# Agent attention with two expert layers: w_in decoded in M's place, decoding begun earlier, keys loaded first, the last block in halves

## The chip, the cores and the metric

The kernel runs on one core of one Trainium2 chip. The metric is the device time of one execution in microseconds (us), as a median of runs. The core has TensorE (matrix products), VectorE (DVE in the rows), ScalarE (ACT), GpSimd (POOL) and SyncE (SP). TensorE writes to PSUM only; 16 DMA engines bring data from the chip's memory, and loads are issued here by SP, by ScalarE or by GpSimd. The clock granted to TensorE has two levels, 1.2 and 2.4 GHz; the profile gives it as a share of the upper one.

## What is computed

The inputs are fp32, but the weights of the expert layers are 64-bit numbers, which the kernel turns into pairs of fp32r numbers (high and low) on the chip. N is 12480 tokens, C is 128 channels, there are 49 agents, and the layers are 2048 wide.

```
a2k = softmax(agents @ k.T / sqrt(128))        # 49 x 12480
agent_v = a2k @ v                              # 49 x 128
x = softmax(q @ agents.T / sqrt(128)) @ agent_v
h = maximum(x @ w_in, 0);   x = (s * h * h + b) @ w_out
h = maximum(x @ w_in2, 0);  out = (h * h) @ w_out2
```

The kernel uses that `x @ w_in` is `softmax(q agents) @ (agent_v @ w_in)`. The 49-row product M = agent_v @ w_in is made once. The high and low parts of the softmax stand in 113 rows of one tile (49 rows, a gap up to row 64, 49 rows), and M stands twice in the same way, so that one product with 113 live rows does both parts.

## The kernel before

The program has a prologue and a main loop. All engines get their instructions in the order in which they are written, and each engine works through its own in that order.

*Loads at the start.* SP loads the agents; ScalarE issues two broadcasts of one number each to 128 partitions, s and b (lines 380 to 382). Then the string `FIRST` (line 24) gives the order of the first loads on SP: `k` is a piece of 1024 keys of 512 KB, `w` a raw block of a weight, also 512 KB, which goes to one of `RAW` = 4 buffers.

*Keys.* There are 13 pieces (the last of 192 keys). In step g of the loop, piece g is transposed on TensorE and copied by ScalarE (`k_transpose`), the load of a later piece is issued, the scores of piece g-1 are made on TensorE and copied by ScalarE (`k_scores`), and a running maximum is taken on VectorE (`k_max`). `KB` = 5 is the number of buffers for keys.

*Decoding.* Each of the four weights has four raw blocks of 512 columns, 16 in all. `w_decode` turns one into a high and a low fp32r tile: one activation on ScalarE reads the raw words, seven instructions follow on VectorE, and a late cast on ScalarE writes the high half. `fill(n)` issues n of these steps, taking two blocks in turn, and when a block is finished it issues the load of a next one on GpSimd's queue. `FILL_K`, `FILL_T`, `FILL_V`, `FM` and `FILL_L` say how many steps stand at which place: per key step, in the softmax's constants, per step of the attention sum, around M's first two pieces, and per step of the main loop. `finish(n)` issues what is missing until n blocks are left.

Here w_in is decoded into the tile of the fourth weight, w_out2 (`wi = wo2_f`). So a block of w_out2 may be decoded only when the piece of M that reads the same columns has been made (`made`).

*Attention sum and M.* 104 products over the key pieces give the sum over v (`ps_av`), while VectorE shifts and ScalarE exponentiates the scores. Then follow in a chain: the reciprocal of the softmax's sum, the scaled sum, its transposition, high and low copies of it (`av`), and M in four pieces of 512 columns (`m_piece`): three products on TensorE, a cast on ScalarE, a subtraction on VectorE. Two pieces stand ahead of the main loop, two in its steps 2 and 3.

*Main loop.* There are 28 blocks of 448 tokens (the last has 384) and eight steps for each block. A step has `up1` (four matmuls with M), `down` of the first layer two steps later, and, eleven steps later, `up2` and the second `down`, six matmuls each. After each `up`, `hidden` does ReLU and square on ScalarE, then the high copy and the low subtraction on VectorE (`split`). The first eleven steps have no second layer yet. At the end of a block, `y2_done` copies the result, `store` transposes it on TensorE, copies it on VectorE and issues the store on SP.

## Time and profile before

| | us |
|---|---|
| runs, three: median (lowest to highest) | 1141.26 (1140.69 to 1141.89) |
| profiled execution | 1140.76 |
| its span in the trace | 1138.8 |
| TensorE busy | 1119.6 |
| VectorE busy | 968.0 |
| ScalarE busy | 944.9 |

The span runs from the first to the last instruction of the trace; the profiled execution's own time is 1.96 us longer. A matmul's busy time includes what overlaps with the next one, so a busy TensorE is not one at its peak. Rows name an instruction by the line of the code, the tile that it writes and the tiles that it reads, and in square brackets the idle time of the engine before it with what ended it.

### The profile page before, as it was taken

How to read it: one execution, taken by the hardware profiler on the slowest of the kernel's cores; microseconds unless marked ns; L12 is line 12 of the kernel's file. 1: busy time of each engine (PE TensorE's matmuls, PEld its weight loads, DVE VectorE, ACT ScalarE, POOL GpSimd, SP SyncE). 2: the span in 40 equal slices, each digit the busy share in tenths (PEclk: the TensorE clock that was granted, in tenths of full speed). 3: DMA queues.
4: the chain of work that ended last, by engine and by line, in shares of the span. 5: the costliest groups of instructions: out<-in, count | busy, mean ns of one | idle time of the engine just before them, and what ended most of it. 6: DMA issues, size and time to landing. Idle time of an engine off the chain costs nothing.

```text
span 1138.8 us, 15466 instructions
## 1 busy us (share of the span) xinstructions
PE 1119.6 (98%) x5787; PEld 1022.8 (90%) x5787; DVE 968.0 (85%) x1426; ACT 944.9 (83%) x1186; POOL 12.7 (1%) x36
## 2 busy tenths in 40 slices
PE   8998999999999999999999999999999999999998
PEld 8886999999999999999999999999999999999997
DVE  4989888888888888888888888888888888888875
ACT  5657888888888888888888888888888888888875
POOL 2110000000000000000000000000000000000000
PEclk8899999999999999999999999999999999999999
DMA  8960019999999999999999999999999999700000
GB/s 318 287 182 1 1 17 8 15 15 15 7 15 15 15 8 15 15 15 10 12 15 15 15 8 15 15 15 8 15 15 15 8 15 15 11 1 9 9 10 15
DMA packets 1282658, 34.96 MB, mean 31 GB/s; under 512 B 1255239, under 2 KB 1277656, under 8 KB 1282584
## 3 DMA queue, kind: packets, MB, share of 16 engines
q1 hardware_dynamic: 1280568, 27.69, 114.4%
q0 software_dynamic: 1728, 6.29, 1.7%
q8 instruction: 45, 0.74, 0.4%
q14 instruction: 29, 0.24, 0.1%
q10 hardware_dynamic: 288, 0.00, 0.0%
HBM read 27.58 MB, written 6.39 MB: 30 GB/s over the span
## 4 chain that ended last, share of the span: by engine, by line
PE 94%; DVE 3%; DMA 1%; issue 1%; ACT 1%; SPq 0%; DVEq 0%; ACTq 0%
PE ps_y L579 47%; PE ps_h L568 24%; PE ps_h L558 15%; PE ps_av L508 2%; PE ps_o L606 1%; PE ps_sT L179 1%; PE ps_ks L426 1%; DMA raw<-in_moe_w_out_dram 1%; DMA kraw<-in_k_dram 1%; DVE gl L115 1%; PE ps_x L225 0%; PE ps_k L416 0%; DVE gh L114 0%; PE ps_b L194 0%; PE ps_s L169 0%
## 5 line engine op out<-in xcount | busy, mean ns | idle before, releaser
L115 DVE TENSOR_TENSOR gl<-r,gh 128x896 fp32r<-128x896 f32 (+1 forms) x448 | 487.4, 1088 | 15.4
L545 ACT ACTIVATE r<-ps_h 128x896 f32<-128x896 f32 (+1 forms) x448 | 408.0, 911 | 110.3 <-PE ps_h L558 90.4
L546 ACT ACTIVATE r<-r 128x896 f32<-128x896 f32 (+1 forms) x448 | 425.9, 951 | 14.2
L114 DVE CAST gh<-r 128x896 fp32r<-128x896 f32 (+1 forms) x448 | 279.2, 623 | 120.7 <-ACT r L546 115.7
L568 PE MATMUL ps_h<-yh,wi2l 128*128 128x448 f32 (+1 forms) x448 | 167.9, 375 | 1.8 <-ACT e L202 1.7
L558 PE MATMUL ps_h<-X,Ml 128*128 128x448 f32 (+1 forms) x448 | 166.1, 371 | 3.0 <-DVE X L236 2.2
L579 PE MATMUL ps_y<-gl,woh 128*128 128x448 f32 (+1 forms) x448 | 164.6, 368 | 0.7 <-DVE gl L115 0.7
L579 PE MATMUL ps_y<-gh,wol 128*128 128x448 f32 (+1 forms) x448 | 164.9, 368 | 0.0
L579 PE MATMUL ps_y<-gl,wo2h 128*128 128x448 f32 (+1 forms) x448 | 163.8, 366 | 0.6 <-DVE gl L115 0.6
L579 PE MATMUL ps_y<-gh,woh 128*128 128x448 f32 (+1 forms) x448 | 164.4, 367 | 0.0
L568 PE MATMUL ps_h<-yh,wi2h 128*128 128x448 f32 (+1 forms) x448 | 163.8, 366 | 0.0
L579 PE MATMUL ps_y<-gh,wo2l 128*128 128x448 f32 (+1 forms) x448 | 163.8, 366 | 0.0
L568 PE MATMUL ps_h<-yl,wi2h 128*128 128x448 f32 (+1 forms) x448 | 163.4, 365 | 0.1
L558 PE MATMUL ps_h<-X,Mh 128*128 128x448 f32 (+1 forms) x448 | 163.5, 365 | 0.0
L579 PE MATMUL ps_y<-gh,wo2h 128*128 128x448 f32 (+1 forms) x448 | 162.4, 362 | 0.0
L558 PEld LDWEIGHTS ps_h<-X,Ml 128*128 128x128 f32 x448 | 84.7, 189 | 11.1 <-issue 3.8
L579 PEld LDWEIGHTS ps_y<-gl,woh 128*128 128x128 f32 x448 | 84.4, 188 | 9.1 <-DVE gl L115 1.2
L579 PEld LDWEIGHTS ps_y<-gh,wol 128*128 128x128 f32 x448 | 84.4, 188 | 8.5 <-ACT y L587 0.4
L579 PEld LDWEIGHTS ps_y<-gl,wo2h 128*128 128x128 f32 x448 | 83.9, 187 | 8.7 <-DVE gl L115 1.2
L568 PEld LDWEIGHTS ps_h<-yh,wi2l 128*128 128x128 f32 x448 | 84.1, 188 | 8.3 <-ACT e L202 2.0
L579 PEld LDWEIGHTS ps_y<-gh,woh 128*128 128x128 f32 x448 | 84.4, 188 | 7.8
L579 PEld LDWEIGHTS ps_y<-gh,wo2l 128*128 128x128 f32 x448 | 83.9, 187 | 8.1 <-ACT oT L598 0.3
(119 smaller groups left out, 976.2 us busy)
## 6 DMA issues: line engine op xcount, KB each, us to landing
kraw<-in_k_dram SPq DMA_DIRECT2D x12, 512.0 KB, 8.3
v<-in_v_dram SPq DMA_DIRECT2D x12, 512.0 KB, 9.6
q_raw<-in_q_dram SPq DMA_DIRECT2D x27, 224.0 KB, 36.3
out_dram<-o SPq DMA_DIRECT2D x27, 224.0 KB, 2.7
raw<-in_moe_w_out_dram POOLq DMA_DIRECT2D x8, 512.0 KB, 7.9
raw<-in_moe_w_in_dram SPq DMA_DIRECT2D x4, 512.0 KB, 8.8
raw<-in_moe_w_in_dram POOLq DMA_DIRECT2D x4, 512.0 KB, 7.0
q_raw<-in_q_dram SPq DMA_DIRECT2D x1, 192.0 KB, 31.6
```

The costliest lines, as they stand in the source:

```text
L114: copy(dst[0], src)
L115: eng_lo.tensor_tensor(out=dst[1], in0=src, in1=dst[0].bitcast(F32), op=ALU.subtract)
L179: nc.tensor.matmul(out=ps[:KS, :n], lhsT=aS, rhs=x[z][:, :n], start=(z == 1), stop=(z == 0))
L426: nc.tensor.matmul(out=sc[:, i], lhsT=x[:, i * p:(i + 1) * p], rhs=aT, start=True, stop=True)
L508: nc.tensor.matmul(out=ps_av[:NA, :C + 1], lhsT=S[:p, t0[g] + i], rhs=vs[g][:p, i], start=(g == 0 and i == 0), stop=(g == NG - 1 and i == ...
L545: nc.scalar.activation(r[:, :, :n], ps[:, :, :n], AF.Relu)
L546: nc.scalar.activation(r[:, :, :n], r[:, :, :n], AF.Square)
L558: nc.tensor.matmul(out=ps[:, c, :n], lhsT=M[z][:, sl], rhs=X[t], start=(z == 1), stop=(z == 0))
L568: nc.tensor.matmul(out=ps[:, c, :n], lhsT=w[:, sl], rhs=y[:, :n], start=(z == 0), stop=(z == 2))
L579: nc.tensor.matmul(out=py[t][:, :n], lhsT=wz[:, m], rhs=g[:, c, :n], start=(m == 0 and z == 0), stop=(m == NCH - 1 and z == 2),)
L606: nc.tensor.transpose(out=po[:, i], in_=x[:, i * p:(i + 1) * p], identity=ident)
```

## The change

- The first loads are `kkwkwkwkwk` instead of `kkwkwkkww`, with six buffers for keys. The agents are loaded on ScalarE's queue. The broadcasts of s and b stand in key step 2, the first loads of q in key step 9 instead of 5.
- `FILL_K` has the same sum, 51, with one step in the first key step and fewer in the last ones, and in each key step the decoding stands ahead of the scores instead of behind the maximum.
- w_in is decoded into M's own tiles, and each piece of M overwrites the columns that it was made from. No block waits for `made` any more. Three more places take decoding steps, `FILL_A` = 1, 2, 2, in the chain from the attention sum to M.
- M's pieces, the softmax tiles X and the matmuls of `up1` take 113 rows instead of 128.
- In the main loop's steps 1, 3, 5, 7 and 9 the high copy of the first layer's hidden tile is made by ScalarE.
- In the last block, the last two hidden tiles of the second layer are worked in two halves, one for each 128 columns of the layer; the result is copied in two halves by ScalarE and VectorE, transposed, copied by both again, and stored on two queues.

```
-KB = 5
-FIRST = "kkwkwkkww"
-FILL_K = (0, 3, 4, 4, 4, 5, 4, 5, 5, 5, 5, 4, 3, 0)
+KB = 6
+FIRST = "kkwkwkwkwk"
+FILL_K = (1, 3, 4, 4, 4, 5, 5, 5, 5, 5, 5, 4, 1, 0)
+HI_ACT = (1, 3, 5, 7, 9)
+FILL_A = (1, 2, 2)
-    av = [const.tile([P, P], F32R, name=f"av{x}") for x in "hl"]
+    av = [const.tile([P, KS], F32R, name=f"av{x}") for x in "hl"]
-    Xs = [const.tile([P, 512], F32R, name=f"X{i}") for i in range(2)]
+    Xs = [const.tile([KS, 512], F32R, name=f"X{i}") for i in range(2)]
-        ex = dec_p.tile([P, WC], I32, tag="ex", name="ex")
+        ex = dec_p.tile([P, WC], I32, tag="ex", name="ex", bufs=2)
-    wi = wo2_f
+    wi = M
...
-                raw, i, pair = loaded[0]
-                if len(to_load) + len(loaded) > NW or i < len(made):
-                    loaded.pop(0)
...
+                raw, i, pair = loaded.pop(0)
+                sl = slice(i * WC, (i + 1) * WC)
+                g = w_decode(raw, pair[0][:, sl], pair[1][:, sl])
...
-            nc.tensor.matmul(out=ps, lhsT=x, rhs=w[:, sl], start=(z == 0), stop=(z == 2))
-        split((M[0][:, sl], M[1][:, sl]), ps, nc.vector, nc.scalar.copy)
-        made.append(i)
+            nc.tensor.matmul(out=ps[:KS], lhsT=x, rhs=w[:, sl], start=(z == 0), stop=(z == 2))
+        split((M[0][:KS, sl], M[1][:KS, sl]), ps[:KS], nc.vector, nc.scalar.copy)
...
-            nc.sync.dma_start(out=ag, in_=agents)
-            nc.scalar.dma_start(out=s_sb, in_=s.partition_broadcast(P))
-            nc.scalar.dma_start(out=b_sb, in_=b.partition_broadcast(P))
+            nc.scalar.dma_start(out=ag, in_=agents)
...
-                if g == KB:
+                if g == 2:
+                    nc.scalar.dma_start(out=s_sb, in_=s.partition_broadcast(P))
+                    nc.scalar.dma_start(out=b_sb, in_=b.partition_broadcast(P))
+                if g == 9:
                     q_load(0)
                     q_load(1)
                 v_upto(min(g - KB, VB))
+                fill(FILL_K[g])
                 if g:
                     k_scores(g - 1)
                 if g > 2:
                     k_max(g - 2)
-                fill(FILL_K[g])
...
             finish(2 * NW)
+            fill(FILL_A[0])
             colsum(0, NW)
...
+            fill(FILL_A[1])
             colsum(NW, 2 * NW)
...
+            fill(FILL_A[2])
             for i in range(2):
                 m_piece(i)
                 fill(FM[i])
...
-        def hidden(ps, n, layer):
+        def hidden(ps, n, layer, copy=nc.vector.tensor_copy, parts=(slice(0, 2),)):
...
-            nc.scalar.activation(r[:, :, :n], ps[:, :, :n], AF.Relu)
-            nc.scalar.activation(r[:, :, :n], r[:, :, :n], AF.Square)
-            split((hi[:, :, :n], lo[:, :, :n]), r[:, :, :n], nc.vector)
+            for c in parts:
+                nc.scalar.activation(r[:, c, :n], ps[:, c, :n], AF.Relu)
+                nc.scalar.activation(r[:, c, :n], r[:, c, :n], AF.Square)
+                split((hi[:, c, :n], lo[:, c, :n]), r[:, c, :n], nc.vector, copy)
...
-                    nc.tensor.matmul(out=ps[:, c, :n], lhsT=M[z][:, sl], rhs=X[t], start=(z == 1), stop=(z == 0))
-            G1[t, i] = hidden(ps, n, 1)
+                    nc.tensor.matmul(out=ps[:, c, :n], lhsT=M[z][:KS, sl], rhs=X[t], start=(z == 1), stop=(z == 0))
+            G1[t, i] = hidden(ps, n, 1, nc.scalar.copy if t * NPR + i in HI_ACT else nc.vector.tensor_copy)
...
+            last = t == NB - 1 and i >= NPR - 2
+            G2[t, i] = hidden(ps, n, 2, parts=(slice(0, 1), slice(1, 2)) if last else (slice(0, 2),))
...
+                nc.scalar.copy(ot[t][:, :n // 2], ps[:, :n // 2])
+                ot[t, 1] = ep.tile([P, 512], F32, tag="oT", name="oT")
+                nc.vector.tensor_copy(ot[t, 1][:, n // 2:n], ps[:, n // 2:n])
...
+            how = ((nc.vector.tensor_copy, nc.sync), (nc.scalar.copy, nc.scalar))
+            for h, (x, (copy, eng)) in enumerate(zip(xs, how)):
+                ps = ps_m.tile([P, 512], F32, tag="m", name="ps_o")
+                po = ps[:p, :jh * C].rearrange("p (j c) -> p j c", c=C)
+                for i in range(jh):
+                    nc.tensor.transpose(out=po[:, i], in_=x[:, (h * jh + i) * p:(h * jh + i + 1) * p], identity=ident)
+                o = ep.tile([P, 4, C], F32, tag="o", name="o")
+                copy(o[:p, :jh], po)
+                eng.dma_start(out=to[:, h * jh:(h + 1) * jh], in_=o[:p, :jh])
```

## Rows read from the trace of the kernel before

**Rows 1.** Page, part 1: busy us, share of span, instructions.
```profile
PE 1119.6 (98%) x5787; PEld 1022.8 (90%) x5787; DVE 968.0 (85%) x1426; ACT 944.9 (83%) x1186; POOL 12.7 (1%) x36
```

**Rows 2.** Busy time by window: length, each engine, granted clock, DMA share, GB/s.
```profile
10.00:20.00 10.00, 10.00 (x70) 10.00 (x70) 5.36 (x12) 5.90 (x9) 0.88 (x1) 0.73 1.03 410
77.00:121.00 44.00, 35.84 (x161) 29.98 (x161) 42.38 (x73) 34.47 (x48) 0.00 (x0) 0.92 0.00 1
121.00:131.00 10.00, 9.85 (x50) 8.86 (x49) 9.29 (x14) 8.89 (x12) 0.00 (x0) 1.00 0.01 2
```

**Rows 3.** The same view, the third and the eighth microsecond.
```profile
2.00:3.00 1.00, 1.00 (x7) 1.00 (x6) 0.00 (x0) 0.95 (x1) 1.00 (x6) 1.00 0.70 67
7.00:8.00 1.00, 0.92 (x8) 0.68 (x7) 0.00 (x0) 0.04 (x1) 0.00 (x0) 1.00 1.01 414
```

**Rows 4.** DMA issues: count, size, us from issue to landing.
```profile
b_sb<-in_moe_b_dram ACTq DMA_DIRECT2D x1, 0.5 KB, 5.9
```

**Rows 5.** Order of time on SP's queue: start, us, what.
```profile
0.74 0.40 SPq L380 DMA_DIRECT2D ag<-in_agents_dram  x1
1.20 0.85 SPq L371 DMA_DIRECT2D kraw<-in_k_dram  x2
```

**Rows 6.** Order of time, TensorE: transposing the second piece of keys.
```profile
8.35 1.75 PE L416 MATMUL ps_k<-ident,kraw 128*128 128x128 f32 x8 [0.43 <-DMA kraw<-in_k_dram]
```

**Rows 7.** Order of time: first decoding on VectorE, and a wait of ScalarE.
```profile
14.54 0.43 DVE L268 TENSOR_SCALAR z<-z 128x512 f32<-128x512 f32 x1 [8.37 <-ACT z L266]
...
35.02 0.69 ACT L266 ACTIVATE z<-raw 128x512 f32<-128x512 f32 x1 [1.75 <-DMA raw<-in_moe_w_out_dram]
```

**Rows 8.** Order of time, VectorE, from the attention sum to M.
```profile
73.35 0.15 DVE L520 TENSOR_SCALAR rs<-ps_av 49x1 f32<-49x1 f32 x1 [1.32 <-PE ps_av L508]
...
75.00 0.33 DVE L530 TENSOR_TENSOR avl<-ps_avT,avh 128x49 fp32r<-128x49 f32 x2 [0.94 <-ACT avh L528]
77.11 0.69 DVE L115 TENSOR_TENSOR Ml<-ps_M,Mh 128x512 fp32r<-128x512 f32 x1 [1.78 <-ACT Mh L114]
```

**Rows 9.** Groups by line and shape, VectorE, 77 to 121 us: busy, mean ns.
```profile
L114 DVE CAST gh<-r 128x896 fp32r<-128x896 f32 x13 | 8.1, 621 | 0.1
L278 DVE SCALAR_TENSOR_TENSOR z<-raw,z 128x512 f32<-128x512 uint32 x4 | 2.7, 686 | 0.0
L271 DVE TENSOR_SCALAR x<-z 128x512 int32<-128x512 int32 x4 | 1.7, 422 | 0.0
```

**Rows 10.** The same view for ScalarE.
```profile
L546 ACT ACTIVATE r<-r 128x896 f32<-128x896 f32 x14 | 13.4, 954 | 0.4
```

**Rows 11.** Chain of waits at the end: start, us, what.
```profile
1128.80 0.82 ACT r L545
...
1130.53 0.57 DVE gh L114
...
1131.12 0.97 DVE gl L115
...
1132.14 1.15 PE ps_y L579 x5
...
1133.31 0.49 ACT oT L598
...
1134.52 0.69 DVE o L608
```

**Rows 12.** Groups by line and shape, weight loads, 300 to 1100 us.
```profile
L606 PEld LDWEIGHTS ps_o<-ident,oT 128*112 128x112 f32 x88 | 10.7, 133 | 2.0
...
L194 PEld LDWEIGHTS ps_b<-ident,sT 113*112 113x112 f32 x38 | 5.1, 134 | 1.5
```

**Rows 13.** Chain of waits in one block of the steady stream.
```profile
329.83 2.47 PE ps_y L579 x12
...
333.11 0.20 PE ps_b L194 x2
...
334.53 2.40 PE ps_y L579 x12
```

More of the change, by code (lines that the diff above doesn't have):

```diff
@@ L299, in next_load @@
             loaded.append((w_load(src, i, eng), i, pair))
-    made, ready, late = [], [], []
+    ready, late = [], []
     undone = [4 * NW]
@@ L309, in fill @@
             if not ready and loaded and (not running or running[-1][1] >= ZA):
-                raw, i, pair = loaded[0]
-                if len(to_load) + len(loaded) > NW or i < len(made):
-                    loaded.pop(0)
-                    sl = slice(i * WC, (i + 1) * WC)
-                    g = w_decode(raw, pair[0][:, sl], pair[1][:, sl])
-                    next(g)
-                    ready.append(g)
+                raw, i, pair = loaded.pop(0)
+                sl = slice(i * WC, (i + 1) * WC)
+                g = w_decode(raw, pair[0][:, sl], pair[1][:, sl])
+                next(g)
+                ready.append(g)
             if not running and ready:
@@ L540, in tile_agent_attention_two_moe @@
         L2 = NPR + LAG + 1
+        NB = len(blocks)
         Y, G1, G2, py1, py2 = {}, {}, {}, {}, {}
-        def hidden(ps, n, layer):
+        def hidden(ps, n, layer, copy=nc.vector.tensor_copy, parts=(slice(0, 2),)):
             r = ep.tile([P, 2, 512], F32, tag="r", name="r")
-            nc.scalar.activation(r[:, :, :n], ps[:, :, :n], AF.Relu)
-            nc.scalar.activation(r[:, :, :n], r[:, :, :n], AF.Square)
             hi = gp.tile([P, 2, 512], F32R, tag=f"gh{layer}", name=f"gh{layer}")
             lo = gp.tile([P, 2, 512], F32R, tag=f"gl{layer}", name=f"gl{layer}")
-            split((hi[:, :, :n], lo[:, :, :n]), r[:, :, :n], nc.vector)
+            for c in parts:
+                nc.scalar.activation(r[:, c, :n], ps[:, c, :n], AF.Relu)
+                nc.scalar.activation(r[:, c, :n], r[:, c, :n], AF.Square)
+                split((hi[:, c, :n], lo[:, c, :n]), r[:, c, :n], nc.vector, copy)
             return hi, lo
@@ L568, in up2 @@
                     nc.tensor.matmul(out=ps[:, c, :n], lhsT=w[:, sl], rhs=y[:, :n], start=(z == 0), stop=(z == 2))
-            G2[t, i] = hidden(ps, n, 2)
+            last = t == NB - 1 and i >= NPR - 2
+            G2[t, i] = hidden(ps, n, 2, parts=(slice(0, 1), slice(1, 2)) if last else (slice(0, 2),))
         def down(t, i, w, G, py, tag):
@@ L597, in y2_done @@
             ot[t] = ep.tile([P, 512], F32, tag="oT", name="oT")
-            nc.scalar.copy(ot[t][:, :n], py2.pop(t)[:, :n])
+            ps = py2.pop(t)
+            if t < NB - 1:
+                nc.scalar.copy(ot[t][:, :n], ps[:, :n])
+            else:
+                nc.scalar.copy(ot[t][:, :n // 2], ps[:, :n // 2])
+                ot[t, 1] = ep.tile([P, 512], F32, tag="oT", name="oT")
+                nc.vector.tensor_copy(ot[t, 1][:, n // 2:n], ps[:, n // 2:n])
         def store(t):
             _, p, j = blocks[t]
-            x = ot.pop(t)
-            ps = ps_m.tile([P, 512], F32, tag="m", name="ps_o")
-            po = ps[:p, :j * C].rearrange("p (j c) -> p j c", c=C)
-            for i in range(j):
-                nc.tensor.transpose(out=po[:, i], in_=x[:, i * p:(i + 1) * p], identity=ident)
-            o = ep.tile([P, 4, C], F32, tag="o", name="o")
-            nc.vector.tensor_copy(o[:p, :j], po)
-            nc.sync.dma_start(out=tokens_of(out, t), in_=o[:p, :j])
-        NB = len(blocks)
+            xs = [ot.pop(t)]
+            if t == NB - 1:
+                xs.append(ot.pop((t, 1)))
+            to = tokens_of(out, t)
+            jh = j // len(xs)
+            how = ((nc.vector.tensor_copy, nc.sync), (nc.scalar.copy, nc.scalar))
[7 more added lines that the diff above has]
+                eng.dma_start(out=to[:, h * jh:(h + 1) * jh], in_=o[:p, :jh])
         total = NB * NPR
```

## The prediction

> **What bounds the kernel now.** I began with the page's busy times: TensorE is busy 98% of a span of 1138.8 us [rows 1]. That share is an average, so the next view is the busy time in windows. From 121 us on TensorE shows 9.85 of 10 us at full clock, and VectorE 9.29; there the matrix stream sets the pace, and only the matmuls' own pitch could change it. Two stretches look otherwise. From 10 to 20 us VectorE is busy 5.36 us of 10 while the granted clock is 0.73, between the two levels of 1.2 and 2.4 GHz. From 77 to 121 us, which is the first eleven steps of the main loop plus the last decoding, VectorE is busy 42.38 of 44 us, TensorE 35.84, ScalarE 34.47 [rows 2]. So there VectorE decides, and whatever it sheds brings the steady stream forward, until ScalarE is as full. Everything after 121 us moves left as a block. The third place is the end: the chain of waits leaves TensorE at 1128.8 us and runs in series through ScalarE, VectorE, TensorE, ScalarE, TensorE and VectorE to 1135.2 us [rows 11]. A gain can come from the start, from 77 to 121 us, and from the end.
>
> **Start and keys.** The first key load is issued at 1.20 us, behind the agents' issue of 0.40 us; on ScalarE's queue the agents free SP at 0.74 us [rows 5]. That is 0.46 us, the low end. The high end: in the third microsecond the DMA engines move 67 GB/s, in the eighth 414 [rows 3], and the broadcast of b, one number to 128 partitions, is in flight meanwhile and lands 5.9 us after its issue [rows 4]. The second keys reach TensorE at 8.35 us [rows 6]. If the small packets are what slows the first loads, two loads of 0.524 MB take 2.5 us at 414 GB/s and start at about 2 us: 4.5 instead of 8.3, so 3.8 us sooner. The slow clock from 10 to 20 us follows TensorE's waits for the first keys; without them up to 2.7 us (0.27 of 10) could come back too. The broadcasts are not gone: they are issued on ScalarE in the third key step and will slow the loads then, when the keys have some lead.
>
> Decoding starts at 14.54 us, after 8.37 us of idle VectorE [rows 7]; the change puts one step before the first scores and the others ahead of each step's scores. The number of steps until the end of the keys stays 51, with four fewer near the end of it (the counts 4, 3 become 4, 1, and 5 come earlier). That only pays if the keys' chain itself ends sooner. Behind a decoding's first ScalarE instruction, which waits for its raw block, now stand the copy of scores and the next copy of keys. At 35.02 us such a wait of 1.75 us is in the trace already [rows 7], since a ring of four raw buffers lets a load go only when an earlier block is through. Reordered, it can vanish or grow by as much. I take 2.5 us for start and keys together, between minus 1 and plus 4.5. It is nearer to the low end of 0.46 + 0 than to 6.5, because VectorE's 51 steps and the ring keep their own pace.
>
> On this the Trainium skill speaks against the change (DMA: Bandwidth & Descriptors, "Issuing engines are not separate DMA queues"): loads from any engine share the same 16 DMA engines, so spreading them saves only the time of issuing. By that rule the part would be worth 0.46 us and the moved broadcasts would cost later what they cost now; rows 3 and 4 show slow loads beside the broadcasts but not which causes which.
>
> **Decoding w_in into M's tiles, and the chain to M.** The fourth weight no longer waits for M, so five steps fit into the chain from the attention sum to M. VectorE idles there 1.32, 0.94 and 1.78 us [rows 8]. One step, two, two: a short one takes 0.42 us, a long one 0.69 [rows 9]; a block has four short and three long, 0.54 on average. The first (0.42) fits into 1.32, the last pair (1.1) into 1.78; the middle pair may run 0.2 us over and delay M by that. So 5 x 0.54 = 2.7 us leave the full stretch, at a price of 0.2.
>
> **Five casts to ScalarE.** For steps 1, 3, 5, 7, 9 the high half is copied by ScalarE: VectorE loses 5 x 0.62 = 3.1 us [rows 9]. ScalarE gains five passes over the same 128x896 at about the square's 0.954 us [rows 10], 4.8 us. VectorE's stretch falls by 5.8 us, to 38.2. ScalarE's work becomes 34.47 + 4.8 less two decoding activations of 0.69 that move ahead [rows 7]: 37.9. The two are then level, and either holds the other through two buffers, so not all of it comes through. If ScalarE kept half of its 9.5 us of idle the stretch would need 42.6 and win 1.4; if nothing is lost, 5.8. I take 4.0, nearer to the upper end, since ScalarE's present idle is mostly spent on waiting for VectorE's backlog and for matmuls that it delays.
>
> **The last block in halves.** Now, after the last up projection at 1128.8: 0.82 and as much again on ScalarE, 0.57 and 0.97 on VectorE, 1.15 on TensorE, 0.49 copy, transposes, 0.69 copy, then the store [rows 11]. A pass of ScalarE over 384 columns takes 0.49 (the copy) where 768 take 0.82. In halves the first column half is ready 0.5 us earlier and its VectorE work lies beside ScalarE's second half. ScalarE does 4 x 0.47 from about 1128.3, to 1130.1; VectorE follows with the second half's 0.35 + 0.55 (estimates: half of 0.57 and 0.97 plus 0.06), to 1131.05; TensorE then owes two matmuls instead of five, to 1131.65 where it was 1133.29 (1132.14 + 1.15). That is 1.65. The copy of 384 columns becomes two of 192 on two engines, about 0.3 instead of 0.49; the last copy, 512 columns in 0.69, becomes two side by side, about 0.4; half the store goes on each queue, from 0 to 0.4 less. Sum 2.2, between 1.2 (if the extra instructions' fixed parts queue up) and 2.8.
>
> **113 rows.** Loading 113 rows by 112 columns takes 134 ns, 128 by 112 takes 133 [rows 12]: rows cost nothing, so I take zero. But the pitch of the stream has two levels: twelve down matmuls take 2.47 or 2.40 us [rows 13], 206 or 200 ns each; in the chain of waits 157 of 202 such pieces between 121 and 1075 us are slow. The fast piece shown follows a transposition of 113 rows. Whether 113 rows in each step keep the stream fast is not in the trace. All fast: 157/202 of 216 steps x 22 matmuls x 5.8 ns = 21 us won; all slow: 6 us lost.
>
> **The sum.** 2.5 + 4.0 + 2.2 = 8.7 us; the 0.2 is inside the 4.0. The profiled execution took 1140.76, which gives 1132.1; the median of the runs, 1141.26, lies 0.5 above it, so I say 1132.5.
>
> **Rivals.**
> The start gives only its issue time (A): 0.46 + 4.0 + 2.2 = 6.7, 1134.6. For it: loads from a cold start may be slow without any broadcast. Against: the rate reaches 414 GB/s just when the broadcast of b lands.
> This is what the Trainium skill's sentence on issuing engines gives, too.
> ScalarE becomes the bound after 77 us (B): 2.5 + 1.4 + 2.2 = 6.1, 1135.2. For it: 37.9 against 38.2 us of work. Against: the casts stand only in every second step, where the neighbour has none.
> 113 rows keep the matmuls at the fast pitch (C): up to 21 us more; half of it, 1122. For: the fast piece behind the 113-row transposition. Against: no 128-column load of 113 rows stands in the trace.
> The other side (D): each passage between 128-row and 113-row matmuls makes the array wait, two per step and 224 steps. The nearest row of it, the slow pitch kept everywhere, costs 6 us and would take the time to 1138.5; from 8.7 us / 448 = 19 ns for each passage the kernel is slower, and at 40 ns it takes 1150. Against: the 113-row transposition stands in the stream at 0.20 for two [rows 13], like any other.
> The Trainium skill states that a change of tiling mode drains TensorE (TensorEngine Tiling (Array Packing), "Key Properties"); its modes are for 64 rows or fewer, and no run here shows one.
> The keys wait for raw blocks (E), and the change's order doesn't do what it should: five waits of 1.75 us, 8.8 in all, would eat the sum: 1141.
>
> **Chances.** Forecast 0.48; A 0.18; B 0.10; C 0.08; D 0.09; E 0.07. Forecast, A, B and C are faster, 0.84; of E half is within 0.2% (2.3 us, about what a measurement of this kernel can tell), a quarter either side, and of D a fifth comes out on the faster side: faster 0.87, same 0.04, slower 0.09. The forecast's own range is 1129 to 1135. For eight in ten I go from 1125.5, where a third of C's 21 us is added to the forecast, to 1138, where D and E begin.
>
> **What would show it.** Right: the second keys at TensorE before 6.5 us; VectorE's first decoding before 11; M's first low half [rows 8] 2 to 3 us before 77.11; VectorE and ScalarE both over 90% busy in the next 38 us; the end of TensorE's last up projection to the last copy's end 4.6 us instead of 6.4; pieces of 2.47 and 2.40 in the old ratio. Wrong: ScalarE idle before a raw block among the keys, two matmul pitches in another mix, or VectorE waiting for ScalarE's cast in the odd steps.

## The result and the profile after

The changed kernel takes 1124.85 us (median of 4 runs, 1124.37 to 1126.51) where the kernel before took 1141.58 in the same comparison (1140.69 to 1144.83): a ratio of 0.985 with a 95% interval of 0.983 to 0.987. It is 16.4 us faster in the spans (1138.8 to 1122.4), where 8.7 were forecast, and the time lies 0.65 us below the range. Times below that come without an interval are of single runs.

Part 1 of the page after, to be read against [rows 1]: TensorE is busy for 13.7 us less, VectorE for 3.7 less, ScalarE for 4.9 more.

```profile
PE 1105.9 (99%) x5787; PEld 1021.1 (91%) x5787; DVE 964.3 (86%) x1426; ACT 949.8 (85%) x1196; POOL 12.4 (1%) x36
```

The number of matmuls is the same, 5787. So part of the gain is not idle time filled: matmuls take less time, because one follows the other sooner or because less of them run at 1.2 GHz. The prediction's sum had none of that. Where each part of the 16.4 us appears is told by four marks, the start of an instruction in both traces:

| stretch | before | after | gain | forecast |
|---|---|---|---|---|
| span's start to the first up projection | 77.95 | 75.28 | 2.7 | 2.5 |
| from there to the 22nd ReLU | 57.87 | 54.36 | 3.5 | 4.0 |
| second block's y copied to the last block's y copied | 964.79 | 956.11 | 8.7 | 0 |
| last matmul of the last up projection to the end | 10.38 | 8.85 | 1.5 | 2.2 |

The first two stretches and the last lie where the prediction put gains, and each came within 0.7 us of it. The third stretch, 208 steps of the steady stream (26 blocks of eight), holds the whole error; "steady stretch" means it from here on. The rows of its ends, copies of y on ScalarE, before and after:

```profile
144.46 0.70 ACT L587 ACTIVATE y<-ps_y,y_bias,s_sb 128x448 f32<-128x448 f32 x1
1109.25 0.65 ACT L587 ACTIVATE y<-ps_y,y_bias,s_sb 128x384 f32<-128x384 f32 x1
```
```profile
138.30 0.71 ACT L592 ACTIVATE y<-ps_y,y_bias,s_sb 128x448 f32<-128x448 f32 x1
1094.41 0.65 ACT L592 ACTIVATE y<-ps_y,y_bias,s_sb 128x384 f32<-128x384 f32 x1
```

What makes it shorter is in the chain of waits. The same view as [rows 13], of the kernel after (start, us, what; `...` stands for rows left out):

```profile
325.17 0.81 PE ps_h L562 x4
...
326.17 1.23 PE ps_h L572 x6
327.40 2.40 PE ps_y L584 x12
...
331.84 2.40 PE ps_y L584 x12
```

Twelve down matmuls in 2.40 us have become the rule; the time from one matmul to the next is called the pitch here. Of the whole pieces of twelve between 121 and 1075 us, 157 of 201 were slow before (2.44 us or more) and 20 of 199 are after; their mean went from 2.456 to 2.406 us (2.408 without three pieces of the shorter last block). That is 0.048 x 208 steps = 10.0 us. The rest of the account comes from adding up, over the whole steady stretch, the times from each matmul's start to the next one's: the down matmuls take 10.0 us less (204.0 ns each before, 199.9 after), the first layer's up projections 1.6 more (204.7 to 206.6 ns), the second layer's 0.6 less, and the products behind the transposed scores (`ps_sT`) 0.5 more. So 8.7 arrive.

The busy time by window, to be read against [rows 2, 3] (the stretches lie 2 us earlier after):

```profile
2.00:3.00 1.00, 1.00 (x7) 1.00 (x6) 0.00 (x0) 0.64 (x1) 1.00 (x6) 1.00 0.72 224
10.00:20.00 10.00, 10.00 (x93) 9.99 (x92) 9.66 (x23) 8.33 (x13) 2.18 (x3) 1.00 0.94 345
75.00:119.00 44.00, 37.48 (x179) 32.35 (x180) 40.81 (x71) 39.83 (x51) 0.00 (x0) 0.96 0.00 1
119.00:129.00 10.00, 10.00 (x51) 9.13 (x50) 9.34 (x13) 9.29 (x12) 0.00 (x0) 1.00 0.00 0
```

In the third microsecond 224 GB/s move instead of 67. From 10 to 20 us VectorE is busy 9.66 us instead of 5.36, and the clock is 1.00 instead of 0.73. From 75 to 119 us ScalarE has become nearly as full as VectorE.

### The profile page after: what moved, and what is told of

It is laid out like the page before. It is cut to its first block, busy times and chain, and to the rows that moved or that the text cites. A ratio compares the mean times of both kernels' runs of the same rounds, so it can differ in the third digit from the quotient of the medians.

```text
span 1122.4 us, 15479 instructions
## 1 busy us (share of the span) xinstructions
PE 1105.9 (99%) x5787; PEld 1021.1 (91%) x5787; DVE 964.3 (86%) x1426; ACT 949.8 (85%) x1196; POOL 12.4 (1%) x36
## 3 DMA queue, kind: packets, MB, share of 16 engines
HBM read 27.58 MB, written 6.39 MB: 30 GB/s over the span
## 4 chain that ended last, share of the span: by engine, by line
PE 93%; DMA 3%; DVE 1%; ACT 1%; issue 0%; SPq 0%; DVEq 0%; ACTq 0%
PE ps_y L584 47%; PE ps_h L572 24%; PE ps_h L562 16%; PE ps_av L507 2%; DMA kraw<-in_k_dram 2%; DMA q_raw<-in_q_dram 2%; PE ps_o L623 1%; PE ps_sT L181 1%; PE ps_x L227 0%; DVE gl L117 0%; PE ps_b L196 0%; PE ps_s L171 0%; ACT r L551 0%; PE ps_q L145 0%; ACT r L552 0%
## 5 line engine op out<-in xcount | busy, mean ns | idle before, releaser
L117 DVE TENSOR_TENSOR gl<-r,gh 128x896 fp32r<-128x896 f32 (+2 forms) x450 | 487.7, 1084 | 16.8 <-ACT gh L116 1.5
L551 ACT ACTIVATE r<-ps_h 128x896 f32<-128x896 f32 (+2 forms) x450 | 408.9, 909 | 98.8 <-PE ps_h L562 79.7
L552 ACT ACTIVATE r<-r 128x896 f32<-128x896 f32 (+2 forms) x450 | 427.0, 949 | 14.3
L116 DVE CAST gh<-r 128x896 fp32r<-128x896 f32 (+2 forms) x445 | 276.7, 622 | 112.5 <-ACT r L552 100.6
L562 PE MATMUL ps_h<-X,Ml 113*128 113x448 f32 (+1 forms) x448 | 166.5, 372 | 2.5 <-DVE X L238 1.7
L562 PE MATMUL ps_h<-X,Mh 113*128 113x448 f32 (+1 forms) x448 | 163.5, 365 | 0.0
L562 PEld LDWEIGHTS ps_h<-X,Ml 113*128 113x128 f32 x448 | 84.3, 188 | 9.3 <-issue 3.3
L572 PEld LDWEIGHTS ps_h<-yl,wi2h 128*128 128x128 f32 x448 | 84.8, 189 | 6.5 <-DVE yl L117 0.2
L572 PEld LDWEIGHTS ps_h<-yh,wi2h 128*128 128x128 f32 x448 | 84.1, 188 | 7.0
L562 PEld LDWEIGHTS ps_h<-X,Mh 113*128 113x128 f32 x448 | 84.9, 190 | 5.2
```

The source lines that it names most:

```text
L116: copy(dst[0], src)
L117: eng_lo.tensor_tensor(out=dst[1], in0=src, in1=dst[0].bitcast(F32), op=ALU.subtract)
L551: nc.scalar.activation(r[:, c, :n], ps[:, c, :n], AF.Relu)
L552: nc.scalar.activation(r[:, c, :n], r[:, c, :n], AF.Square)
L562: nc.tensor.matmul(out=ps[:, c, :n], lhsT=M[z][:KS, sl], rhs=X[t], start=(z == 1), stop=(z == 0))
L572: nc.tensor.matmul(out=ps[:, c, :n], lhsT=w[:, sl], rhs=y[:, :n], start=(z == 0), stop=(z == 2))
```

## Experiments

### The steady stream: 113 rows, or something else?

Three kernels take the 113 rows apart. One returns the first product to 128 rows in the changed kernel, one puts the 113 rows alone into the kernel before, one keeps the change but makes `av` 128 columns wide again.

```
a_rows128 (from after)
+    Xs = [const.tile([P, 512], F32R, name=f"X{i}") for i in range(2)]
+    ... lhsT=M[z][:, sl], rhs=X[t] ...
b_rows113 (from before)
+    Xs = [const.tile([KS, 512], F32R, name=f"X{i}") for i in range(2)]
+    ... lhsT=M[z][:KS, sl], rhs=X[t] ...
a_av128 (from after)
+    av = [const.tile([P, P], F32R, name=f"av{x}") for x in "hl"]
+    ... lhsT=x[:, :KS] ...   # m_piece
```

> The changed kernel, but the up projections with M run over 128 rows again; rows 113 to 127 of X are zero, those of M hold leftover decoded weights, so the output is the same. Every tile keeps its address. Theory R (the 113 live rows keep the stream at the fast pitch): the mean pitch of the down matmuls in the steady stream goes back from 200.4 and 200.2 ns to about 205.3 and 204.1, and the time rises by 8 to 10 us, to 1133 to 1135. Theory P (another placement of tiles in SBUF does it): the pitch stays at 200 and the time at 1124 to 1126. Theory O (the pitch follows from the order of work or from when the loop begins): the same as P, 1124 to 1126.

Measured: 1124.9 us, ratio to before 0.986 (0.984 to 0.988), which is the changed kernel's. Its steady stretch takes 956.9 us, between these copies of y; 38 of 201 pieces are slow.

```profile
138.40 0.71 ACT L592 ACTIVATE y<-ps_y,y_bias,s_sb 128x448 f32<-128x448 f32 x1
1095.27 0.65 ACT L592 ACTIVATE y<-ps_y,y_bias,s_sb 128x384 f32<-128x384 f32 x1
```

How far one trace of this stretch can be trusted is told by nine kernels of this document that have the changed kernel's code and places in it (the changed kernel itself, and those of the last three sections of the experiments): they lie between 956.1 and 957.1 us, with 20 to 33 slow pieces. So 956.9 is not told from the changed kernel's, and the rows are not what the changed kernel gains by.

> The kernel before with one part of the change alone: the up projections with M take 113 rows, and X has 113 rows. Theory R: the down matmuls' mean pitch falls from 205.3 and 204.1 to about 200.5, and the time falls by 8 to 10 us, to 1131 to 1133; first up projection, end of the keys and the tail stay where they were. Theories P and O: pitch 205 and 204 and time 1140.5 to 1142 as before.

Measured: 1137.07 us, ratio 0.997 (0.995 to 0.999). The steady stretch takes 960.8 instead of 964.8 us, and 97 of 202 pieces are slow. In the kernel before, the rows are worth 4.0 us. Two answers that don't agree: 4.0 there, at most 0.8 here. Something else in the change must do the same work.

> The changed kernel with the two av tiles 128 columns wide again, of which 113 are read, so that every tile allocated behind them lies 120 bytes further along its partition, as it does before the change. Theory P: pitch of the down matmuls 204 to 205, time 1133 to 1135. Theories R and O: pitch 200.2 to 200.5, time 1124 to 1126.5.

Measured: 1130.22 us and a steady stretch of 960.8, that of b_rows113, with 96 of 202 pieces slow; the time lies between what the theories expected. No instruction of the steady stream differs from the changed kernel's. What differs is where its tiles lie. The constant tiles are laid one behind the other in SBUF, the memory in which all tiles lie that are not in PSUM, and a partition of `av` takes 452 bytes (480 with rounding) instead of 512; two of them shift all that is allocated later by 64 bytes (not by 120, as the expectation has it): w_out, w_in2, w_out2, X and the hidden tiles of the main loop.

The straight test is the kernel before with that shift and nothing else: an unused tile of 192 bytes ahead of `wo`, which leaves the tiles behind it at the same place within 256 bytes as in the changed kernel.

```
b_pad192 (from before)
+    const.tile([P, 48], F32, name="pad0")
     wo = [const.tile([P, NCH, C], F32R, name=f"wo{x}") for x in "hl"]
```

> The kernel before with nothing changed but an unused tile of 192 bytes per partition ahead of the second and later weights, so that all tiles from there on stand, modulo 256 bytes, where they stand in the changed kernel (64 bytes less than 256 further). 128 rows everywhere. Theory P (placement alone sets the pitch): mean pitch of the down matmuls 201.3 and 200.8 ns as with the changed kernel at 128 rows, instead of 205.3 and 204.1, and the time 8 us less than before, 1132 to 1134. Rival (placement acts only together with the changed order of work): pitch over 203, time 1137 to 1142.

Measured: 1134.42 us, ratio 0.993 (0.991 to 0.995), from a tile that nobody uses. The chain of waits of this kernel (two of the down matmuls' pieces), and the ends of its steady stretch:

```profile
325.85 2.40 PE ps_y L580 x12
...
330.85 2.40 PE ps_y L580 x12
```
```profile
147.25 0.71 ACT L588 ACTIVATE y<-ps_y,y_bias,s_sb 128x448 f32<-128x448 f32 x1
1103.16 0.65 ACT L588 ACTIVATE y<-ps_y,y_bias,s_sb 128x384 f32<-128x384 f32 x1
```

24 of 199 pieces are slow and the steady stretch takes 955.9 us, 8.9 less than before and as little as the changed kernel's. (The median gains less, 7.2, and in the profile the first up projection comes 2.8 us later than before, after a longer time at 1.2 GHz among the keys.) The four corners are then: old place and 128 rows 964.8, old place and 113 rows 960.8, new place and 128 rows 956.9 (955.9 in the padded kernel), new place and 113 rows 956.1. At the new place the stretch takes 956 to 957 us with or without the rows: the place alone gives the gain of 8.7 us.

### Which tiles, and which place?

Pads of 32 to 224 bytes move one group of tiles at a time. In the kernel before the groups start at these bytes within 256: M 128, the three weights 224, X 192, the hidden tiles 128. In the changed kernel: 128, 160, 128, 64. Each edit of this section adds unused tiles ahead of the groups that it moves, in the form of b_pad192, to the changed kernel.

| | M | weights | X | hidden | steady stretch, us |
|---|---|---|---|---|---|
| before | 128 | 224 | 192 | 128 | 964.8 |
| after | 128 | 160 | 128 | 64 | 956.1 |
| p_X: X back | 128 | 160 | 192 | 64 | 960.9 |
| p_W: weights back | 128 | 224 | 128 | 64 | 969.8 |
| p_G: hidden back | 128 | 160 | 128 | 128 | 964.0 |
| p_all128 | 128 | 128 | 128 | 128 | 962.1 |
| r_shift: all by 64 | 192 | 224 | 192 | 128 | 959.0 |
| r_W64: weights at 128 | 128 | 128 | 128 | 64 | 957.9 |

> The changed kernel with unused bytes before and after the softmax tiles X, so that X alone starts where it did before the change (192 instead of 128, modulo 256 bytes); all other tiles stay, modulo 256. The steady stretch between the second and the last evacuation of the first layer lasts 964.8 us before, 956.1 in the changed kernel. If X's place is what sets the pitch: 960 to 965; if not: 956 to 957.

> The same for the three decoded weights w_out, w_in2, w_out2 alone: start 224 instead of 160, modulo 256, as before the change; M, X and the hidden tiles stay. If the weights' place sets the pitch: the steady stretch takes 960 to 965 us; if not: 956 to 957.

> The same for everything behind X, above all the hidden tiles gh and gl and the tiles yh and yl that stream through TensorE: start 128 instead of 64, modulo 256, as before the change; M, X and the weights stay. If the place of the streamed tiles sets the pitch: 960 to 965 us; if not: 956 to 957. If each of the three single moves stays at 956 to 957, it is a relation of two of them, or the 113 rows and the placement only act together.

> The changed kernel with unused bytes so that M, the other weights, X and all streamed tiles start at the same place, 128 modulo 256. If starting at a multiple of 128 bytes is what counts (weights now start at 160): the up matmuls' mean pitch falls from 203.7 towards 200 too and the steady stretch to 948 to 953 us; if the difference between tiles counts and equal starts are bad: 960 to 970; if neither: 955 to 957.

Measured: 1129.12, 1138.14, 1130.65 and 1128.29 us. Each of the three groups matters, and the weights most: moved back alone they cost 13.7 us. All three moved back together, which is the placement of a_av128, cost 4.7, so the groups don't add. Equal starts for all groups (p_all128) cost 6.0. In p_W 199 of 199 pieces are slow:

```profile
324.60 2.46 PE ps_y L586 x12
...
329.31 2.46 PE ps_y L586 x12
```

That only the distances between the groups decide, not the place itself, was the next theory. r_shift keeps all distances of the changed kernel, r_W64 changes those of the weights alone.

> The changed kernel with every tile that feeds TensorE in the main loop moved by the same 64 bytes (192, 224, 192, 128 modulo 256 for M, the other weights, X and the streamed hidden tiles). Theory D (the pitch follows from the distance between the weights being loaded and the tile being streamed): nothing changes, steady stretch 955.9 to 957. Theory S (the place itself counts, each tile against a boundary of 128 or 256 bytes): 960 to 970, since these are nearly the places of the kernel before with X moved.

> The changed kernel with the three decoded weights 32 bytes nearer to the streamed tiles: distance 64 modulo 256 instead of 96 (distances tried so far: 96 gives a steady stretch of 956.1, 0 gives 962.1, 32 gives 964.0, 160 gives 969.8). Theory D: another value again, and by the trend between 32 and 96 from 955 to 962. If it is under 955.5 it is a better placement than the changed kernel's.

Measured: 1127.33 us and 1125.59 us. With every distance kept, r_shift loses 2.9 us in the steady stretch, and r_W64, with another distance, only 1.8. In r_W64 the pieces even have a third length, 2.43 us, all alike but for those of the shorter last block:

```profile
326.14 2.43 PE ps_y L586 x12
...
330.59 2.43 PE ps_y L586 x12
```

The distances alone don't decide. It is shown that the place where the tiles start sets the pitch, 13.7 us from the best to the worst of this table; by what rule stays open. The rows of the table after the first two are single traces.

### The start

The changed kernel's start has four edits: the agents on another queue, the broadcasts of s and b two key steps later, more loads issued ahead, and the decoding ahead of the scores. The last two were not tested alone. One kernel moved the broadcasts back behind the agents (and left the last block whole), one moved the agents alone back to SP, one both.

```
a_sb0_whole (from after)
             nc.scalar.dma_start(out=ag, in_=agents)
+            nc.scalar.dma_start(out=s_sb, ...); nc.scalar.dma_start(out=b_sb, ...)
             # ... and not in key step 2
+            last = False        # and the last block copied and stored whole
a_agsp (from after)
-            nc.scalar.dma_start(out=ag, in_=agents)
+            nc.sync.dma_start(out=ag, in_=agents)
a_start (from after)
-            nc.scalar.dma_start(out=ag, in_=agents)
+            nc.sync.dma_start(out=ag, in_=agents)
+            nc.scalar.dma_start(out=s_sb, ...); nc.scalar.dma_start(out=b_sb, ...)
             # ... and not in key step 2
```

> The changed kernel with two parts undone in stretches far from each other: the broadcasts of s and b are issued at the start again (on ScalarE's queue, behind the agents), and the last block is worked whole. Start: theory S (the broadcasts' small packets slow the first key loads): second keys at TensorE at 7.8 to 8.3 us instead of 6.4 to 7.0, a slow clock among the first keys as before, and the first up projection at 76 to 78. Rival C (the first loads are slow by themselves and only SP's issue counts): second keys at 6.4 to 7.2. End: from the start of the last up projection's last matmul to the end of the span 10.4 us as before instead of 8.85; so 1.5 us of the 2.2 forecast.

Measured: 1126.82 us. The second keys came at 6.99 us, not at 8.35, which seemed to acquit the broadcasts; but they were issued later here than in the kernel before, behind the agents, and then it was the third piece of keys that came late (11.95 us instead of 9.49). The rate falls just ahead of it, in the sixth microsecond, to 82 GB/s:

```profile
11.95 1.06 PE L414 MATMUL ps_k<-ident,kraw 128*128 128x128 f32 x8 [1.65 <-DMA kraw<-in_k_dram]
```
```profile
5.00:6.00 1.00, 1.00 (x6) 0.91 (x6) 0.45 (x3) 0.00 (x0) 0.00 (x0) 1.00 0.39 82
```

The end with a whole last block took 10.37 us, so the halves are worth 1.5.

> The changed kernel with the agents loaded on SP's queue ahead of the keys again, the broadcasts of s and b still in the third key step. If it is the agents' place that decides (the keys' loads leave 0.46 us later), the second keys reach TensorE at 6.85 us or later, instead of 6.39, and by the upper case, that the agents' 49 rows hold the queue, at 8.35 as before. If it is the broadcasts, the second keys stay between 6.4 and 6.9 us, and the last key score between 39.7 and 40.2 us.

> The changed kernel with the whole start of before: the agents on SP, the broadcasts of s and b on ScalarE's queue ahead of everything. If the broadcasts' 256 small packets are what holds the first loads, the second keys reach TensorE at 8.0 to 8.4 us, as before (8.35), while the kernel with the agents alone on SP stays below 7. If only the issue counts, both have the second keys at about 6.9 us. The last key score then comes 1.5 to 2.5 us later than the changed kernel's 39.66 by the first theory, 0.5 later by the second.

Measured: 1125.35 us and 1127.52 us. The order of time on TensorE and the busy time by window of a_agsp, the agents alone moved back:

```profile
5.23 2.39 PE L412 MATMUL ps_k<-ident,kraw 128*128 128x128 f32 x16
```
```profile
3.00:4.00 1.00, 1.00 (x7) 1.00 (x6) 0.00 (x0) 0.00 (x0) 1.00 (x3) 1.00 0.93 373
```

and the same of a_start:

```profile
7.06 1.09 PE L414 MATMUL ps_k<-ident,kraw 128*128 128x128 f32 x8 [1.76 <-DMA kraw<-in_k_dram]
8.40 1.68 PE L414 MATMUL ps_k<-ident,kraw 128*128 128x128 f32 x8 [0.24 <-DMA kraw<-in_k_dram]
```
```profile
3.00:4.00 1.00, 1.00 (x7) 1.00 (x6) 0.00 (x0) 0.00 (x0) 1.00 (x3) 1.00 0.34 70
```

With the agents on SP both first loads of keys are there by 6.6 us. With the broadcasts at the start too, the rate falls from 373 to 70 GB/s in the fourth microsecond, and the second keys come at 8.40 us, as before [rows 6]. The first up projection starts at 75.28 us after, at 75.36 in a_agsp, at 77.57 in a_start. So, with the agents on SP, the broadcasts' place is worth 2.2 us, and with the broadcasts moved the agents' queue is worth 0.1: two transfers of one number each, to 128 partitions, hold up the first megabyte. The delay itself is clear: the third keys come at 13.18 us in a_start and at 9.2 to 10.1 in every kernel with the broadcasts moved. The sizes at the first up projection are those of single traces, and a_nohi and a_rows128, which have the changed kernel's code up to there, start it at 74.79 and 75.53, so 0.1 is not told from nothing. With the broadcasts at the start it did matter where the agents stood: a_sb0_whole, whose agents go ahead of them on ScalarE's queue, starts it at 76.24, 1.3 us before a_start. The Trainium skill's rule that the issuing engine saves only the issuing (DMA: Bandwidth & Descriptors, "Issuing engines are not separate DMA queues") agrees with the 0.1 us. The same page says of transfers under 64 KB that one pays mostly overhead ("Rules for kernel authors"); the broadcasts, 0.5 KB each, took 5.9 us for b [rows 4].

### Between the keys and the attention sum

After the last key score, the attention sum starts 6.84 us later in the changed kernel, 5.62 before. The chain of waits names the loads of q, which now are issued in key step 9 (start, us, what):

```profile
25.04 16.86 DMA q_raw<-in_q_dram
...
42.04 0.59 PE ps_q L145 x4
```

```
a_q5, a_q7 (from after)
+                if g == 5:      # a_q7: if g == 7
                     q_load(0)
                     q_load(1)
```

> The changed kernel with the first two loads of q issued in key step 5, as before the change, instead of step 9. Theory Q (between the last key score, 39.66 us, and the first product of the attention sum, 46.50, the changed kernel waits for q, which costs 1.2 us of the 3.7 won among the keys): first product at 45.0 to 45.5 and the time 1 to 1.5 us less, 1123 to 1124. Rival (the softmax constants on VectorE set that stretch): first product at 46.3 to 46.7, the time 1124 to 1126.5. Should the earlier q loads delay the keys, the end of the keys moves from 39.66 to 40 or later and nothing is won.

Measured: 1128.68 us. The wait for q is gone (5.66 us from the last key score to the sum), but the last key score came at 44.61 instead of 39.66 us: what q gains the keys lose, and more.

> The changed kernel with the first two loads of q in key step 7, right behind the last keys, instead of step 9. From the last key score to the attention sum's first product: 5.6 us as before the change instead of 6.6 to 7.7, and the keys end as in the changed kernel, at 38.5 to 40: 1 to 1.5 us less, 1123.3 to 1124 as median. Rival (the keys are delayed as with step 5, to over 41, or the first v now lands late): no gain, 1124.5 to 1127.

Measured: 1125.18 us, ratio 0.985 (0.983 to 0.987), the changed kernel's. The wait fell to 5.84 us, the keys ended 1.3 us later, and the first up projection started at 75.24 instead of 75.28. No version tried is clearly faster than the changed kernel.

### From the first up projection to the full stream

Three kernels leave out the five decoding steps in the chain to M (`FILL_A`; the same steps come later), the five casts on ScalarE (`HI_ACT`), or both.

```
a_nofill:  FILL_A = (0, 0, 0)
a_nohi:    HI_ACT = ()
a_both:    FILL_A = (0, 0, 0); HI_ACT = ()
```

> The changed kernel without the five decoding steps in the chain to M. Same stretch, first up projection to 22nd ReLU: theory V: 56 to 57 (five steps of 0.54 come back on VectorE), while the chain from the end of the attention sum to the first up projection, 4.9 us, becomes 4.6 to 4.9. Rival (there is slack): 54.2 to 55.2 and the time within 1 us of the changed kernel.

> The changed kernel with all high copies of the hidden tiles on VectorE again (no step casts on ScalarE). The stretch from the first up projection to the 22nd ReLU takes 54.4 us in the changed kernel and 57.9 in the one before. Theory V (VectorE is the bound there, five casts of 0.62 count): 56.5 to 57.5. Rival A (ScalarE is as full, so the casts bring little): 54.2 to 55.2.

> The changed kernel with both undone, the five casts on ScalarE and the five decoding steps in the chain to M. One alone undone: stretch from first up projection to 22nd ReLU 55.84 (casts) and 58.98 (steps) against 54.36. Theory V (VectorE alone bounds the stretch, the costs add): 1.5 + 4.6 = 6.1 more, 60.5. Rival (ScalarE is the bound when both its casts and the late decoding fall into the same steps): 57.0 to 58.5, as the kernel before (57.87), that is less than with the steps alone undone.

Measured: 1129.74, 1125.43 and 1129.44 us, and 58.98, 55.84 and 59.53 us to the 22nd ReLU; none lies in a range that was expected. In the first of them the clock was at its lower level for twice as long as in the others early in this stretch, so it is compared with none. The busy time by window, from the first up projection to the 14th ReLU, for before, a_both, a_nohi, a_q7 and after:

```profile
77.95:119.07 41.12, 33.76 (x150) 28.15 (x151) 40.00 (x71) 31.63 (x43) 0.00 (x0) 0.92 0.00 1
```
```profile
74.67:117.36 42.69, 34.87 (x155) 28.67 (x156) 40.07 (x71) 30.75 (x42) 0.00 (x0) 0.92 0.00 1
```
```profile
74.79:113.72 38.93, 33.05 (x148) 27.90 (x149) 37.59 (x65) 29.92 (x40) 0.00 (x0) 0.91 0.00 1
```
```profile
75.24:114.36 39.12, 32.78 (x150) 28.31 (x151) 34.78 (x61) 33.99 (x44) 0.00 (x0) 0.91 0.00 1
```
```profile
75.28:112.79 37.51, 31.42 (x150) 26.98 (x151) 34.78 (x61) 34.02 (x44) 0.00 (x0) 0.95 0.00 1
```

The second column, the length, makes a ladder. From a_both to a_nohi the five steps in the chain bring 3.8 us. From a_nohi to a_q7, which has the changed kernel's code in this stretch, the casts on ScalarE take 2.8 us of work from VectorE (37.59 to 34.78) and the stretch gets 0.2 us longer. From a_q7 to after, the same instructions with the same busy times take 1.6 us less, and only the granted clock differs. The part of the stretch in which it differs, a_q7 and then after:

```profile
95.00:100.00 5.00, 3.26 (x16) 2.72 (x16) 4.89 (x8) 4.63 (x7) 0.00 (x0) 1.00 0.00 0
100.00:105.00 5.00, 5.00 (x25) 4.49 (x23) 4.86 (x10) 3.17 (x5) 0.00 (x0) 0.66 0.00 0
```
```profile
95.00:100.00 5.00, 3.27 (x17) 2.74 (x16) 4.89 (x9) 4.60 (x7) 0.00 (x0) 1.00 0.00 0
100.00:105.00 5.00, 5.00 (x31) 4.38 (x30) 4.87 (x9) 4.57 (x6) 0.00 (x0) 1.00 0.00 0
```

TensorE did the same before, 3.3 of 5 us busy at 2.4 GHz. In one kernel the clock then fell to 1.2 GHz for a time, in the other it didn't. The code of this stretch does not decide it alone: of fourteen kernels here with the same steps twelve had one fall of the clock in it and took 37.5 to 37.6 us (p_all128 38.1), a_q7 and r_shift had two and took 39.1. But the six kernels without the steps, the casts or both (before, b_rows113, b_pad192, a_both, a_nofill, a_nohi) all had two (granted clock 0.88 to 0.92 over the stretch, against 0.95 or 0.96 with one), and in a_nohi TensorE was busy for only 2.76 us from 95 to 100. So the casts may earn the 1.6 us by keeping TensorE busier; one trace of a_nohi does not show it, and it stays open. The first step of the ladder, from before to a_both, costs 1.6 us with VectorE's work equal; a_both decodes in another order, and what that costs was not taken apart.

## Why the prediction was wrong

**The step that failed: "Everything after 121 us moves left as a block".** With it the steady stream counted for nothing in the sum, and the one term that might have changed it, 113 rows, was put at zero: "rows cost nothing, so I take zero". The stream holds 8.7 us where the sum missed 7.7 (the other terms together were 1.0 too high). What the runs showed in its place: the narrower `av` moves the weights, X and the hidden tiles by 64 bytes, and this shift alone, in the kernel before, takes 8.9 us off the steady stretch (b_pad192). No term of the prediction had a tile's place in it. One of its signs of being wrong, "two matmul pitches in another mix", is what came.

The row under the zero was read rightly: loading 113 rows by 128 columns takes 189 ns, loading 128 rows 188. This is the view of [rows 12], of the kernel after:

```profile
L562 PEld LDWEIGHTS ps_h<-X,Mh 113*128 113x128 f32 x386 | 72.9, 189 | 4.4
...
L572 PEld LDWEIGHTS ps_h<-yh,wi2l 128*128 128x128 f32 x386 | 72.6, 188 | 5.6
```

The Trainium skill has it so too (TensorE: Matmul & The Clock Gate, "LDWEIGHTS (loading the stationary operand)": the columns count, not the rows), and the two lines agree: 189 and 188 ns. A load's duration did not tell the stream's pitch, though: in the kernel before, the rows are worth 4.0 us. In the changed kernel they add 0.8 at most, so that zero was nearly right for them there is luck. [Rows 13] had shown two pitches for one and the same instruction, and the prediction asked only whether the number of rows would choose between them. That the edit of `av` moves every later tile was visible in the diff and was not asked.

**Rival C**, half the stream at the fast pitch, gave 1122 and came nearest, by luck: its reason is mostly not the one that acted. The rows alone do work that way in the kernel before (4.0 us, 157 slow pieces to 97). In the changed kernel they add 0.8 us at most. The up projections never got the fast pitch that its 21 us also counted (206.6 ns each in the first layer, 207.2 in the second). **Rival D**, a price for each passage between 128 and 113 rows, is out: with the passages alone b_rows113 gets faster.

**Start, 2.5 forecast, 2.7 measured: right, and by the upper end's mechanism.** The second keys come at 6.39 us (below 6.5 was expected; 6.1 to 7.0 in kernels with the same code up to there), VectorE's first decoding at 8.20 (below 11). The broadcasts are the main cause; A falls, as the agents' queue gives 0.1. How near the number came is partly luck: kernels that differ from the changed one in the place of tiles alone start the first up projection between 72.68 us (p_all128) and 76.51 (a_av128). Of the 3.7 us by which the keys end sooner 1.2 go to the wait for q. (The counts of decoding steps near the keys' end fell by two, 4 and 3 to 4 and 1, not by four as the prediction has it.) ScalarE's waits for raw blocks, in order of time, to be read against [rows 7]:

```profile
22.98 0.66 ACT L268 ACTIVATE z<-raw 128x512 f32<-128x512 f32 x1 [3.49 <-DMA raw<-in_moe_w_out_dram]
...
33.48 0.68 ACT L268 ACTIVATE z<-raw 128x512 f32<-128x512 f32 x1 [1.52 <-DMA raw<-in_moe_w_out_dram]
```

The waits for raw blocks that rival E feared exist: six, 7.0 us in all, where the kernel before had three, 2.2 in all. The keys end sooner all the same, since the chain of waits among them goes through the keys' own loads:

```profile
8.67 14.93 DMA kraw<-in_k_dram
```

**The chain to M: right, and free.** Order of time on VectorE, against [rows 8]: the chain from its first instruction to M's low half takes 3.76 us in both kernels, though in the changed one four of the five decoding steps lie in it and the fifth just ahead.

```profile
70.69 0.15 DVE L520 TENSOR_SCALAR rs<-ps_av 49x1 f32<-49x1 f32 x1 [1.33 <-PE ps_av L507]
...
71.33 0.67 DVE L275 SCALAR_TENSOR_TENSOR x<-z,x 128x512 int32<-128x512 int32 x1
71.93 0.68 DVE L285 SCALAR_TENSOR_TENSOR wi2l<-z,ex 128x512 fp32r<-128x512 f32 x1
...
74.45 0.69 DVE L117 TENSOR_TENSOR Ml<-ps_M,Mh 113x512 fp32r<-113x512 f32 x1 [0.94 <-ACT Mh L116]
```

**After M, 4.0 forecast, 3.5 measured: the sum right, its terms not.** Up to the 14th ReLU the five decoding steps were worth 3.8 against 2.7, the casts at the same clock nothing against 3.1; 1.6 came from the clock, and 1.6 went with the other order of decoding (3.8 - 0.2 + 1.6 - 1.6 = 3.6). That the sum came out near 4.0 is luck. The casts did what they should: five of them cost ScalarE 4.7 us, and both engines are over 90% busy (34.78 and 34.02 of 37.51). The two groups by line, VectorE and ScalarE, against [rows 9, 10]:

```profile
L116 DVE CAST gh<-r 128x896 fp32r<-128x896 f32 x10 | 6.2, 624 | 0.8 <-ACT r L552 0.8
```
```profile
L116 ACT CAST gh<-r 128x896 fp32r<-128x896 f32 x5 | 4.7, 942 | 0.2
```

That fits rival B, for this one term: VectorE sheds 0.62 us and ScalarE takes 0.94 in the same chain from ReLU to the low half. That this is why the stretch got no shorter is argued, not shown.

**The end, 2.2 forecast, 1.5 measured.** ScalarE on the last two tiles, and the copies, against [rows 11]:

```profile
1112.82 0.47 ACT L551 ACTIVATE r<-ps_h 128x384 f32<-128x384 f32 x1
1113.33 0.53 ACT L552 ACTIVATE r<-r 128x384 f32<-128x384 f32 x1
1113.95 0.49 ACT L551 ACTIVATE r<-ps_h 128x384 f32<-128x384 f32 x1
...
1115.41 0.53 ACT L552 ACTIVATE r<-r 128x384 f32<-128x384 f32 x1
1117.63 0.32 ACT L607 COPY oT<-ps_y 128x192 f32<-128x192 f32 x1 [1.70 <-PE ps_y L584]
```
```profile
1117.98 0.36 DVE L609 COPY oT<-ps_y 128x192 f32<-128x192 f32 x1 [1.07 <-ACT oT L607]
1118.47 0.42 DVE L625 COPY o<-ps_o 96x256 f32<-96x256 f32 x1
```

The first half was to start 0.5 us before the last matmul's end. It could not: until 1113.86 ScalarE worked on the tile before, also halved. From the last up matmul's start to the last down matmul's end it takes 4.04 us instead of 4.86, a gain of 0.8 where the prediction had 1.65. The two copies of the result, meant to run side by side, run one after the other: VectorE's waits for ScalarE's. With that the copies and transposes give 0.3. The store, on two queues, gives 0.4.

## What to carry to other kernels

Before a change is priced, ask what it moves in SBUF: a constant tile made shorter shifts every tile behind it, and here that was worth 8.7 us, more than the 7.7 of all that the change was written for. When one instruction shows two pitches in a trace, find out what chooses between them first, for instance with an unused tile of 32 to 224 bytes, an edit of one line. And a pass moved from a fuller engine to a less full one need not gain anything: here, in one chain on both engines, it gained nothing at the same clock.

## What was not expected of the hardware

- The pitch of an fp32r matmul over 448 columns depended on where its operands start in SBUF: from start to start the mean of the down matmuls lies between 199.9 ns (after) and 204.8 ns (p_W), and the steady stretch between 955.9 and 969.8 us, for moves of 32 to 224 bytes. The Trainium skill's price for back-to-back matmuls of N columns (TensorE: Matmul & The Clock Gate, "Wait — 56ns, not 53.3ns?", N by 2.4 GHz and about 2.5 ns) would give 189 ns, an estimate; the lowest of these means is 199.9.
- 113 rows of contraction instead of 128 change the pitch of the matmuls that follow (157 of 201 slow pieces to 97 of 202) at one placement and hardly at the other (38 slow pieces of 201 to between 20 and 33), while the loads of weights take the same time.
- The clock fell in one kernel and stayed up in another after 25 us of the same instructions with the same busy times (a_q7 and after); it was worth 1.6 us here.
- Two broadcasts of one number, at the head of ScalarE's queue, cut the first loads from 373 to 70 GB/s in the fourth microsecond and delayed the first up projection by 2.2 us (a_agsp to a_start, 1125.35 and 1127.52 us in single runs).
